# Wider loads for batch 1, later expert weights and additive masks in a fused attention and maxout kernel

## The chip, the cores and the metric

The kernel runs on one core of one Trainium2 chip. The metric is the device time of one execution in microseconds (us), and a version counts as faster or slower when it differs by more than 2%. Two runs of the kernel before took 212.20 and 213.75 us, median 212.97. A profile of one execution comes with each version; its span is 1.7 to 2.1 us shorter than the time of the same execution. The mean TensorE clock that was granted over the span is given as a share of full speed; its record begins only with the first change that it notes, at about 18 us in the changed kernel, and the stretch before counts as full.

Names used throughout: PE is the matmul engine (TensorE), PEld its weight loads, DVE is VectorE, ACT is ScalarE, POOL is GpSimd, SP is SyncE, which in this kernel issues every DMA. In the dense layer xs is the attention's result by tokens and xt its transpose; qb and qk are q and k of a pair before and after their transpose.

## The reference

Attention over 4 batches of 8 heads, 768 tokens, head dimension 64. Three heads are full causal ones, five keep only 4 sink tokens and a window of 64. The result, put together to 3072 rows of 512, goes through a dense layer with two experts, whose elementwise maximum is projected back.

```python
scores = scale * np.matmul(q, k.transpose(0, 1, 3, 2))        # q, k, v: (4, 8, 768, 64) float32
stream_keep = causal & (is_sink | in_win)                     # 4 sinks, window 64
mask = np.where(retr[0, :, 0, 0, None, None], full_mask, stream_mask)
scores = np.where(mask[None, :, :, :], scores, -1000000000.0)
scores = scores - np.max(scores, axis=-1, keepdims=True)
a = np.exp(scores)
a = a / (np.sum(a, axis=-1, keepdims=True) + 1e-09)
attn_out = np.matmul(a, v)
x = attn_out.transpose(0, 2, 1, 3).reshape(B * S, H * D)      # (3072, 512)
h1 = x @ w1                                                   # w1, w2: (512, 1024)
h2 = x @ w2
g = np.maximum(h1, h2)
out = g @ w_out                                               # w_out: (1024, 512)
```

The inputs q and k are drawn with a standard deviation of 0.1; this matters once below.

## The kernel before

The kernel works on pairs of heads: four pairs for each batch, sixteen in all, and after each batch's four pairs the dense layer of that batch ("dense(b)"). The dense layer uses max(h1, h2) = h2 + relu(x(w1 - w2)), so it needs `wd` = w1 - w2 and a product `wm` = w2 w_out that is computed once.

The kernel carries a scheduler of its own, `Plan`. Each operation is declared with a cost for each engine that may run it, its dependencies, its buffers, and a priority. `Plan.schedule` plays these costs through once while the program is built, and the order it finds is the fixed order in which each engine then runs its instructions. Engines run in order: if the next instruction is not ready, those behind it wait too (PE's wait of 3.58 us below is a case).

The buffers that matter here:

```python
    ld_t = tl("ld", [128, 2, NB, D], F32, 9)      # landing buffers of q, k, v
    qb_t = tl("qb", [128, 2, NB, 2, D], BF16, 3)  # q, k cast to bf16
    qk_t = tl("qk", [128, 2, S], BF16, 3)         # q, k transposed
    ...
    gt_t = [old(2, 1, FC, GT), old(0, 0, FC, GT), old(0, 1, FC, GT)]
    ot_t = tl("ot", [128, d_model], F32, 3)       # finished output tiles, waiting for their store
    sc_t = psum("sc", 2, 2)
    po_t = psum("po", 2)
    mm_t = psum("mm", 2)                          # PSUM of dense tiles and transposes
```

A pair loads q, k, v, casts q and k, and transposes them. Batch 0 transposes on PE; the others use a DMA transpose. The "(p n)" order gives each partition six tokens in a row (1536 bytes in one piece); "(n p)" gives pieces of one token (256 bytes).

```python
                order, rate = ("(p n)", 0.34) if b == 0 and src is not v else ("(n p)", 0.225)
                ...  # two loads of src, "o {order} d -> p (o n) d"
                cast.append(P.op(f, {"POOL": 0.95, "DVE": 0.62} if r < 1 else {"POOL": 0.95}, loads[i],
                                 [raws[i], qb], prio=r + 0.01 * i))
                if b > 0:
                    continue
                ...  # PE transposes of qb into PSUM, copied to qk by DVE or ACT
            if b > 0:
                tk.append(P.op(lambda e: nc.sync.dma_start_transpose(
                    out=qk.t.rearrange("c i (n p) -> c (i n) p", p=128),
                    in_=qb.t.rearrange("p i n h d -> p (i n h d)")),
                    {"SP": XBAR}, cast, [qb, qk], prio=r - 0.5, size=0.393, rate=0.2))
```

The exponentiated scores are masked by DVE multiplies, in every batch. `wd` is computed by POOL or DVE:

```python
                    if not pointer:
                        def mk(e, a=a, h0=h0, nh=nh, kind=kind, diag=diag):
                            for x, m in mask_pieces(kind, diag, a.t[:, h0:h0 + nh], nh, s0 + h0):
                                V.tensor_mul(out=x, in0=x, in1=m)
            ...
            def f(e, c=c):
                (V if e == "DVE" else nc.gpsimd).tensor_sub(
                    out=wd_bf[:, c, :], in0=w_raw[0][:, c, :], in1=w_raw[1][:, c, :])
            wd_ops.append(P.op(f, {"DVE": 1.3, "POOL": 2.4}, [d_w["w1", c], d_w["w2", c]], prio=48 + c))
```

The dense layer of batches 1 to 3 gets its input by DMA transposes, and each output tile goes from PSUM to an `ot` tile and from there to DRAM, both transposes and stores issued on the same SP queue as the loads:

```python
                    xt_ops[b].append(P.op(lambda e, n0=n0, n1=n1: nc.sync.dma_start_transpose(
                        out=xt[b].t[:, n0:n1].rearrange("c n k p -> c (n k) p"),
                        in_=xs[b].t[:, n0:n1].rearrange("p n d -> p (n d)")),
                        {"SP": XBAR}, norms[b], [xs[b], xt[b]], prio=-5, size=0.393, rate=0.2))
    ...
                    bk, ot = Buf(mm_p), Buf(ot_p)
                    ...  # twelve matmuls into bk
                    o = P.op(lambda e, bk=bk, ot=ot: copy(e, ot.t, bk.t[:, 0]), {"ACT": 0.53, "DVE": 0.69}, [o],
                             [bk, ot], prio=16 + b)
                    P.op(lambda e, ot=ot, r0=r0: nc.sync.dma_start(out=out[r0:r0 + 128, :], in_=ot.t),
                         {"SP": 0.45}, [o], [ot], prio=-10, size=0.262, rate=0.3)
```

## Time and profile before

| | before |
|---|---|
| time, two runs | 212.20 and 213.75 us |
| profiled span, mean granted clock | 211.9 us, 0.932 |
| PE busy | 176.6 us (83%) |
| first PE matmul / first matmul of dense(0) | 13.46 / 56.6 us |
| batch 1's two xt transposes issued | 105.28 and 107.76 us |
| first matmul of dense(1) | 111.2 us |
| last PE matmul ends | 204.8 us |

First the page of the kernel before, in part: busy time of the engines, then the span in 40 equal slices of 5.3 us, each digit the busy share in tenths; PEclk is the granted clock in tenths.

```profile
PE 176.6 (83%) x1460; PEld 94.4 (45%) x1460; DVE 80.1 (38%) x202; ACT 115.9 (55%) x196; POOL 68.2 (32%) x161
...
PE   0038864689799999997879999999999999999960
...
PEclk9999996599999999999556999999999999999995
DMA  5999999999999999999999999951183202112030
...
DMA packets 99118, 38.91 MB, mean 184 GB/s; under 512 B 91920, under 2 KB 93968, under 8 KB 99088
```

Two things can be read off. The DMA row stands at 9 from 5 us until about 138 us: the input stream is saturated for two thirds of the span. And PE is full only where its row shows 9 at full clock; counting slices from 0, there are two holes after PE's start, slices 5 to 10 (27 to 58 us) and 18 to 20 (95 to 111 us), and in or just after both the clock falls to half as well.

The windows view of PE says how much work is missing there. Its columns are the stretch, its length, PE busy time (instructions), granted clock, DMA share and GB/s.

```profile
10.00:20.00 10.00, 5.11 (x39) 1.00 1.14 320
...
30.00:40.00 10.00, 3.69 (x39) 0.65 1.11 261
...
100.00:110.00 10.00, 7.46 (x73) 0.56 1.28 230
110.00:120.00 10.00, 9.70 (x57) 0.75 1.14 230
```

The first hole is made on other engines. The timeline around 29 us (start, duration, engine, line, operation, in brackets the idle time before and what ended it):

```profile
28.82 0.22 DVE L505 TENSOR_TENSOR at<-at,tri 128x128 bf16<-128x128 bf16 x1
...
29.26 6.96 POOL L386 TENSOR_TENSOR wd_bf<-raw 128x1024 bf16<-128x1024 f32 x3
...
29.65 4.33 DVE L505 TENSOR_TENSOR at<-at,tri 128x128 bf16<-128x128 bf16 x2
...
34.04 0.23 PE L514 MATMUL po<-vb,at 128*128 128x65 bf16 x1 [1.78 <-DVE at L505]
```

While POOL subtracts weights, two mask multiplies of a form that took 0.22 us just before take 4.33 us together, and PE waits for them. The second hole belongs to the queue. The timeline of SP, which issues all DMAs in order:

```profile
105.28 1.80 SPq L628 DMA_TRANSPOSE xt<-xs  x1
107.18 0.53 SPq L686 DMA_DIRECT2D out_dram<-ot  x1
107.76 1.47 SPq L628 DMA_TRANSPOSE xt<-xs  x1
```

Dense(1) cannot start before these two transposes have landed, and until it starts PE has only short attention work. From 111.2 us PE is full to its end at 204.8.

### The profile page before, as it was taken

To read this page: it belongs to the slowest core of one execution; us is meant where nothing else is said; L and a number is where in the kernel's file an instruction comes from. 1 tells how busy PE (TensorE), PEld (TensorE's weight loads), DVE (VectorE), ACT (ScalarE), POOL (GpSimd) and SP (SyncE) were. 2 spreads that over 40 slices of the span, in tenths; PEclk is the share of its full clock that TensorE was granted. 3 is DMA by queue.
4 is the path that set the end of the run, shared out by engine and by line. 5 is a ranking of instruction groups with operands and counts; after the bars stand their busy time and mean duration, and the time that the engine had idled before them with its cause. 6 is when DMAs were issued, how large, how long until landed. Compare 5 with 4: busy or idle time off the path is not lost.

```text
span 211.9 us, 4178 instructions
## 1 busy us (share of the span) xinstructions
PE 176.6 (83%) x1460; PEld 94.4 (45%) x1460; DVE 80.1 (38%) x202; ACT 115.9 (55%) x196; POOL 68.2 (32%) x161
## 2 busy tenths in 40 slices
PE   0038864689799999997879999999999999999960
PEld 0024641545445446545455454545554554545420
DVE  6523799935524563515662035364700000000000
ACT  2088894137385875649553476878472442725320
POOL 6007769929801476243282406120000000000000
PEclk9999996599999999999556999999999999999995
DMA  5999999999999999999999999951183202112030
GB/s 167 404 321 314 357 391 246 221 200 227 209 180 209 236 178 247 242 203 225 192 260 235 232 180 218 212 120 54 49 152 101 99 0 99 53 49 99 14 114 34
DMA packets 99118, 38.91 MB, mean 184 GB/s; under 512 B 91920, under 2 KB 93968, under 8 KB 99088
## 3 DMA queue, kind: packets, MB, share of 16 engines
q1 hardware_dynamic: 99088, 38.55, 82.2%
q8 instruction: 13, 0.21, 0.4%
q14 instruction: 17, 0.14, 0.2%
HBM read 25.17 MB, written 6.29 MB: 148 GB/s over the span
## 4 chain that ended last, share of the span: by engine, by line
PE 69%; DVE 8%; ACT 4%; issue 4%; DVEq 0%; ACTq 0%
PE mm L655 15%; PE mm L673 12%; PE po L514 6%; PE sc L479 6%; PE mm L679 6%; PE po L673 5%; PE sc L655 3%; PE mm L406 3%; DVE at L505 3%; PE po L655 2%; PE po L679 2%; PE sc L673 2%; DVE as_all L505 2%; ACT at L497 2%; ACT as_all L497 2%
## 5 line engine op out<-in xcount | busy, mean ns | idle before, releaser
L497 ACT ACTIVATE at<-sc 128x1024 bf16<-128x1024 f32 (+3 forms) x48 | 33.7, 743 | 7.1 <-PE sc L479 6.5
L655 PE MATMUL mm<-xt,wd_bf 128*128 128x384 bf16 x180 | 35.1, 338 | 0.1
L273 POOL CAST qb<-ld 128x384 bf16<-128x384 f32 x60 | 32.1, 573 | 3.8 <-DMA ld<-in_q_dram 2.0
L655 PEld LDWEIGHTS <-wd_bf 128*128 128x128 bf16 x256 | 24.8, 100 | 18.9 <-issue 4.3
L497 ACT ACTIVATE as_all<-sc 128x896 bf16<-128x896 f32 (+5 forms) x36 | 24.5, 711 | 8.9 <-PE sc L479 8.7
L673 PE MATMUL mm<-wo_bf,raw 128*128 128x512 bf16 x120 | 29.4, 379 | 0.0
L273 POOL CAST vb<-ld 128x384 bf16<-128x384 f32 x32 | 16.2, 533 | 38.6 <-PE po L514 17.1
L505 DVE TENSOR_TENSOR as_all<-as_all,smk 128x384 bf16<-128x384 bf16 (+4 forms) x44 | 20.8, 498 | 20.6 <-ACT as_all L497 20.1
L479 PE MATMUL sc<-qk 64*128 64x192 bf16 (+4 forms) x216 | 25.0, 295 | 2.9 <-ACT as_all L497 1.2
L673 PEld LDWEIGHTS <-raw 128*128 128x128 bf16 x192 | 17.7, 98 | 19.6 <-issue 0.7
L662 ACT ACTIVATE raw<-mm 128x384 bf16<-128x384 f32 x37 | 18.2, 493 | 12.5 <-PE mm L655 11.5
L505 DVE TENSOR_TENSOR at<-at,tri 128x256 bf16<-128x256 bf16 (+1 forms) x48 | 17.1, 364 | 17.4 <-ACT at L497 17.3
L514 PE MATMUL po<-vb,at 128*128 128x65 bf16 x252 | 15.8, 204 | 4.3 <-DVE at L505 4.3
L271 ACT COPY ot<-mm 128x512 f32<-128x512 f32 x14 | 8.2, 587 | 19.8 <-PE mm L679 17.4
L538 DVE TENSOR_TENSOR xs<-po,rz 128x384 f32 x32 | 17.8, 557 | 1.5 <-DVE rz L537 0.4
L582 PE MATMUL mm<-ident,qb 128*128 128x128 bf16 x48 | 5.4, 268 | 14.2 <-DVE qb L273 13.8
L479 PEld LDWEIGHTS <-qk 64*128 64x128 bf16 x216 | 9.3, 97 | 16.7 <-issue 12.8
L514 PEld LDWEIGHTS <-at 128*128 128x128 bf16 x252 | 11.5, 104 | 11.5 <-DVE at L505 7.0
L514 PE MATMUL po<-vb,as_all 128*128 128x65 bf16 x220 | 13.3, 206 | 3.4 <-DVE as_all L505 3.3
L679 PE MATMUL mm<-wm_bf,xt 128*128 128x512 bf16 x60 | 15.4, 380 | 0.0
L514 PEld LDWEIGHTS <-as_all 128*128 128x128 bf16 x220 | 10.5, 105 | 8.9 <-DVE as_all L505 4.8
L679 PEld LDWEIGHTS <-xt 128*128 128x128 bf16 x96 | 8.7, 98 | 9.9 <-issue 0.4
(75 smaller groups left out, 169.4 us busy)
## 6 DMA issues: line engine op xcount, KB each, us to landing
ld<-in_q_dram SPq DMA_DIRECT2D x32, 192.0 KB, 4.3
ld<-in_k_dram SPq DMA_DIRECT2D x32, 192.0 KB, 4.3
ld<-in_v_dram SPq DMA_DIRECT2D x32, 192.0 KB, 4.2
out_dram<-ot SPq DMA_DIRECT2D x24, 256.0 KB, 2.0
raw<-in_moe_w_dram SPq DMA_DIRECT2D x8, 512.0 KB, 7.8
raw<-in_moe_w_out_dram SPq DMA_DIRECT2D x4, 512.0 KB, 5.4
qk<-qb SPq DMA_TRANSPOSE x12, 4.9
xt<-xs SPq DMA_TRANSPOSE x6, 3.8
```

The costliest lines, as they stand in the source:

```text
L271: nc.scalar.copy(out=o, in_=i)
L273: (V if e == "DVE" else nc.gpsimd).tensor_copy(out=o, in_=i)
L406: nc.tensor.matmul(bk.t[:, 0], lhsT=w2t[:, f, c * 128:(c + 1) * 128], rhs=wo_bf[:, f, :], start=(f == 0), stop=(f == FC - 1))
L479: nc.tensor.matmul(sc.t[:, h, off:off + w], lhsT=qk.t[64 * h:64 * h + 64, 1, j * 128:(j + 1) * 128], rhs=qk.t[64 * h:64 * h + 64, 0, q0:q0 ...
L497: nc.scalar.activation(out=view(a.t[:, h:h + m]), in_=view(sc.t[:, h:h + m]), func=ACT.Exp, scale=scale, bias=0.0 if bias is None else bia ...
L505: V.tensor_mul(out=x, in0=x, in1=m)
L514: nc.tensor.matmul(po[h].t[:, 0, i * (D + 1):(i + 1) * (D + 1)], lhsT=a.t[:, h, off + t * 128:off + (t + 1) * 128], rhs=vb.t[:, h, j, :], ...
L538: V.tensor_tensor(out=xs[b].t[:, :, bass.ds(col(s0 + h), D)], in0=p3[:, :, 0:D], in1=rz.t.unsqueeze(2).to_broadcast([128, NB, D]), op=ALU. ...
L655: nc.tensor.matmul(bk.t[:, 0, 0:GT], lhsT=wd_bf[:, c, f * 128:(f + 1) * 128], rhs=xt[b].t[:, g * NB // NG:(g + 1) * NB // NG, c, :], start ...
L662: nc.scalar.activation(out=gt.t[:, f, :], in_=bk.t[:, 0, 0:GT], func=ACT.Relu)
L673: nc.tensor.matmul(bk.t[:, 0], lhsT=gt.t[:, f, t * 128:(t + 1) * 128], rhs=wo_bf[:, f, :], start=(f == 0), stop=False)
L679: nc.tensor.matmul(bk.t[:, 0], lhsT=xt[b].t[:, c0 // 128, c, :], rhs=wm_bf[:, c, :], start=False, stop=(c == KC - 1))
```

## The change

The intent is to take work off the saturated DMA queue and off the engines that starve PE early on:

- Batch 1's q and k load in 1536-byte rows as batch 0's do, and are transposed on PE; four of the twelve DMA transposes of q and k disappear.
- w2 leaves the front of the queue. w1 and w2 load in column halves, w1 behind pair 3, and dense(0)'s first half needs only the first half of `wd`.
- Batch 0's masks are added in PSUM: after the score matmuls, a matmul of the identity with a tile of large negative numbers adds to the scores what the exponential turns to zero. Batch 0 then needs no mask multiplies on DVE.
- Smaller: batch 0's casts may run on DVE, one of the three `gt` buffers gets memory of its own, and some costs and priorities that the planner uses are new.

The core of the diff (cuts marked with three dots):

```diff
+WIDE, NARROW = 0.33, 0.215
+WIDE_TO, MASK_TO, X_BAR = 2, 1, 1
...
-    gt_t = [old(2, 1, FC, GT), old(0, 0, FC, GT), old(0, 1, FC, GT)]
+    gt_t = [tl("gt", [128, FC, GT]), old(2, 1, FC, GT), old(0, 0, FC, GT)]
...
+    def quarter(c):
+        return (slice(c % 2 * KC // 2, (c % 2 + 1) * KC // 2), slice(c // 2 * d_ff // 2, (c // 2 + 1) * d_ff // 2))
+
-    EARLY = (("wo", 0), ("wo", 1), ("wo", 2), ("wo", 3), ("w2", 0), ("w2", 1))
+    EARLY = (("wo", 0), ("wo", 1), ("wo", 2), ("wo", 3))
+    LATER = {("w2", 0): 1.5, ("w2", 1): 1.51, ("w2", 2): 1.52, ("w2", 3): 1.53,
+             ("w1", 0): 3.5, ("w1", 1): 3.51, ("w1", 2): 3.52, ("w1", 3): 3.53}
...
+                by_pe = exact and b < MASK_TO
...
-                                                 start=True, stop=True, skip_group_check=True)
+                                                 start=i == 0, stop=not by_pe, skip_group_check=True)
...
+                def drop(e, hs=hs, steps=steps, sc=sc, score=score):
+                    score(e)
+                    for h in hs:
+                        kind, _, n, diag = steps[h]
+                        for o, m in negatives(kind, diag):
+                            nc.tensor.matmul(sc.t[:, h, o:o + m.shape[-1]], lhsT=ident, rhs=m,
+                                             start=False, stop=True, skip_group_check=True)
...
-                    if not pointer:
+                    if not pointer and not by_pe:
                         def mk(e, a=a, h0=h0, nh=nh, kind=kind, diag=diag):
...
-                order, rate = ("(p n)", 0.34) if b == 0 and src is not v else ("(n p)", 0.225)
+                order, rate = ("(p n)", WIDE) if b < WIDE_TO and src is not v else ("(n p)", NARROW)
...
-                if b > 0:
+                if b >= WIDE_TO:
                     continue
...
-            if b > 0:
+            if b >= WIDE_TO:
                 tk.append(P.op(lambda e: nc.sync.dma_start_transpose(
```

`WIDE_TO` and `MASK_TO` are the number of batches with wide loads and with masks in PSUM.

More of the change, by code (lines that the diff above doesn't have):

```diff
@@ L19 @@
     __slots__ = ("emit", "cost", "deps", "bufs", "prio", "size", "rate", "left", "users",
-                 "ready", "engine", "start", "end", "done", "rows", "then")
+                 "ready", "engine", "start", "end", "done", "rows", "rows_after", "then")
     def __init__(self, emit, cost, deps, bufs, prio, size, rate):
@@ L28, in __init__ @@
         self.engine = self.start = self.end = self.done = None
-        self.rows, self.then = 128, None
+        self.rows, self.rows_after, self.then = 128, None, None
 class Buf:
@@ L70, in schedule @@
         clock = dict.fromkeys(ready, 0.0)
-        dma = 0.0
+        dma = DMA_START
         rows = 128
@@ L123, in schedule @@
                 o.end += SWITCH if o.rows != rows else 0.0
-                rows = o.rows
+                rows = o.rows_after or o.rows
             clock[e] = o.end
@@ L154, in u_engine_differs @@
     return o.size or list(u.cost) != [e]
-W_PRIO = 2.5
-XBAR = 2.6
+XBAR = 2.4
+DMA_START = 0.0
+WIDE, NARROW = 0.33, 0.215
+WIDE_TO, MASK_TO, X_BAR = 2, 1, 1
 @with_exitstack
@@ L231 @@
     bias_0 = tl("bias_0", [128, H], F32)
-    warm = tl("warm", [128, 1], F32)
     tri = tl("tri", [128, 128])
     smk = tl("smk", [128, 448 + 320])
+    ntri = rel[:, 0:64].bitcast(BF16)
+    nsmk = tl("nsmk", [128, 448 + 320])
     w2_bf = tl("w2_bf", [128, KC, d_ff])
@@ L275, in load_weight @@
     def load_weight(name, c):
-        dst, arr, n = {"w1": (w_raw[0], moe_w1, KC // 4), "w2": (w_raw[1], moe_w2, KC // 4),
-                       "wo": (w_raw[2], moe_w_out, FC // 4)}[name]
-        nc.sync.dma_start(out=dst[:, c * n:(c + 1) * n, :],
-                          in_=arr[c * 128 * n:(c + 1) * 128 * n, :].rearrange("(c p) f -> p c f", p=128))
-    EARLY = (("wo", 0), ("wo", 1), ("wo", 2), ("wo", 3), ("w2", 0), ("w2", 1))
+        dst, arr = {"w1": (w_raw[0], moe_w1), "w2": (w_raw[1], moe_w2), "wo": (w_raw[2], moe_w_out)}[name]
+        if name == "wo":
+            rows, cols = slice(c * FC // 4, (c + 1) * FC // 4), slice(0, d_model)
+        else:
+            rows, cols = quarter(c)
+        nc.sync.dma_start(out=dst[:, rows, cols],
+                          in_=arr[rows.start * 128:rows.stop * 128, cols].rearrange("(c p) f -> p c f", p=128))
+    def quarter(c):
[3 more added lines that the diff above has]
+             ("w1", 0): 3.5, ("w1", 1): 3.51, ("w1", 2): 3.52, ("w1", 3): 3.53}
     with tc.manual_schedule():
@@ L291 @@
         V.memset(one, 1.0)
-        nc.scalar.activation(out=warm, in_=one[:, 0:1], func=ACT.Exp, scale=1.0, bias=0.0)
+        nc.scalar.activation(out=nsf[:, 0:1], in_=one[:, 0:1], func=ACT.Exp, scale=1.0, bias=0.0)
         V.tensor_scalar(out=ident, in0=rel[:, 0:128], scalar1=0.0, scalar2=None, op0=ALU.is_equal)
@@ L357, in f @@
                 V.tensor_copy(out=smk[:, 576:768], in_=smk[:, 256:448])
-            c_m = P.op(f, {"DVE": 1.0}, prio=-20)
+                for m, o in ((tri, ntri), (smk, nsmk)):
+                    V.tensor_scalar(out=o, in0=m, scalar1=1.0, scalar2=-NEG, op0=ALU.subtract, op1=ALU.mult)
+            c_m = P.op(f, {"DVE": 1.8}, prio=-20)
         else:
@@ L371, in run @@
         d_w = {}
-        for i, name in enumerate(("w2", "w1")):
+        for name in ("w2", "w1"):
             for c in range(4):
@@ L375, in run @@
                     lambda e, name=name, c=c: load_weight(name, c), {"SP": 0.5},
-                    prio=W_PRIO + 0.1 * i + 0.01 * c, size=0.524, rate=0.36)
+                    prio=LATER[name, c], size=0.524, rate=0.35)
         wd_ops, w2_ops, wo_ops, wm_ops, w2t_ops = [], [], [], [], []
         for c in range(4):
-            w2_ops.append(P.op(lambda e, c=c: copy(e, w2_bf[:, c, :], w_raw[1][:, c, :]),
+            w2_ops.append(P.op(lambda e, c=c: copy(e, w2_bf[(slice(None),) + quarter(c)], w_raw[1][(slice(None),) + quarter(c)]),
                                {"DVE": 0.62, "ACT": 0.95}, [d_w["w2", c]], prio=40 + c))
@@ L385, in f @@
             def f(e, c=c):
-                (V if e == "DVE" else nc.gpsimd).tensor_sub(
-                    out=wd_bf[:, c, :], in0=w_raw[0][:, c, :], in1=w_raw[1][:, c, :])
-            wd_ops.append(P.op(f, {"DVE": 1.3, "POOL": 2.4}, [d_w["w1", c], d_w["w2", c]], prio=48 + c))
+                at = (slice(None),) + quarter(c)
+                (V if e == "DVE" else nc.gpsimd).tensor_sub(out=wd_bf[at], in0=w_raw[0][at], in1=w_raw[1][at])
+            wd_ops.append(P.op(f, {"DVE": 1.3, "POOL": 2.4}, [d_w["w1", c], d_w["w2", c]], prio=30 + c))
         for fch in range(FC):
@@ L396, in tr @@
                                         w2_bf[:, c, fch * 128:(fch + 1) * 128], ident)
-            o = P.op(tr, {"PE": 0.23}, w2_ops, [bk], prio=300 + fch)
+            o = P.op(tr, {"PE": 0.23}, w2_ops[2 * (fch // 4):2 * (fch // 4) + 2], [bk], prio=300 + fch)
             w2t_ops.append(P.op(lambda e, fch=fch, bk=bk: copy(e, w2t[:, fch, :], bk.t[:, 0].bitcast(BF16)[:, 0:d_model]),
@@ L449, in mask_pieces, with negatives @@
             return []
+        def negatives(kind, diag):
+            if kind == "tri":
+                return [(o, ntri) for o in diag]
+            if kind == "band1":
+                return [(256 * m, nsmk[:, 256:448]) for m in range(2)]
+            return [(0, nsmk[:, 0:448] if kind == "band0" else nsmk[:, 448:768])]
         def attend(b, p, qk, vb, tk, ov, sink, r):
@@ L481, in score @@
                                                  rhs=qk.t[64 * h:64 * h + 64, 0, q0:q0 + w],
-                                                 start=True, stop=True, skip_group_check=True)
+                                                 start=i == 0, stop=not by_pe, skip_group_check=True)
                 cols = max(sum(g[2] for g in steps[h][1]) for h in hs)
-                so = score_op(score, cols / 2400 + 0.01, tk, [qk, sc], pr)
-                so.rows = 64
+                def drop(e, hs=hs, steps=steps, sc=sc, score=score):
[5 more added lines that the diff above has]
+                                             start=False, stop=True, skip_group_check=True)
+                extra = sum(m.shape[-1] for h in hs for o, m in negatives(steps[h][0], steps[h][3])) if by_pe else 0
+                so = score_op(drop if by_pe else score, cols / 2400 + 0.01 + (extra / 2400 + SWITCH if by_pe else 0),
+                              tk + ([c_m] if by_pe else []), [qk, sc], pr)
+                so.rows, so.rows_after = 64, 128 if by_pe else 64
                 ready = {}
@@ L544, in tok @@
             return t.rearrange("c (p n) -> c p n", n=NB)
-        def blk(t):
-            return t.rearrange("c (n p) -> c p n", p=128)
         def pair(b, p):
@@ L572, in f @@
                         copy(e, qb.t[:, i, :, h, :], raws[i].t[:, h])
-                cast.append(P.op(f, {"POOL": 0.95, "DVE": 0.62} if r < 1 else {"POOL": 0.95}, loads[i],
+                cast.append(P.op(f, {"POOL": 0.95, "DVE": 0.62} if b == 0 else {"POOL": 0.95}, loads[i],
                                  [raws[i], qb], prio=r + 0.01 * i))
-                if b > 0:
+                if b >= WIDE_TO:
                     continue
@@ L584, in pair @@
                 o = P.op(tr, {"PE": 0.34}, [cast[i]], [qb, bk, qk], prio=90 + 2 * r)
-                tk.append(P.op(lambda e, bk=bk, i=i: copy(e, tok(qk.t[:, i]), blk(bk.t[:, 0].bitcast(BF16)[:, 0:S])),
+                tk.append(P.op(lambda e, bk=bk, i=i: copy(
+                    e, tok(qk.t[:, i]), bk.t[:, 0].bitcast(BF16)[:, 0:S].rearrange("c (n p) -> c p n", p=128)),
                                {"DVE": 0.95, "ACT": 0.8}, [o], [bk, qk], prio=r))
-            if b > 0:
+            if b >= WIDE_TO:
                 tk.append(P.op(lambda e: nc.sync.dma_start_transpose(
@@ L594, in fv @@
                     copy(e, vb.t[:, h, :, 0:D], raws[2].t[:, h])
-            ov = P.op(fv, {"POOL": 0.95}, loads[2],
+            ov = P.op(fv, {"POOL": 0.95, "DVE": 0.7} if b == 0 else {"POOL": 0.95}, loads[2],
                       [raws[2], vb], prio=r + 0.05)
@@ L624, in x_turn @@
         def x_turn(b):
-            if b > 0:
+            if b >= X_BAR:
                 for g in range(NG):
@@ L657, in up @@
                                              start=(c == 0), stop=(c == KC - 1))
-                    o = P.op(up, {"PE": 0.65}, (xt_ops[b][g:g + 1] if b > 0 else xt_ops[b]) + wd_ops + wo_ops, [bk, gt, xt[b]], prio=1000 + 100 * b + 10 * g)
+                    o = P.op(up, {"PE": 0.65}, (xt_ops[b][g:g + 1] if b >= X_BAR else xt_ops[b]) +
+                             (wd_ops[2 * (f // 4):2 * (f // 4) + 2] + wo_ops if b == 0 else wd_ops + wo_ops + w2t_ops), [bk, gt, xt[b]], prio=1000 + 100 * b + 10 * g)
                     def relu(e, f=f, bk=bk, gt=gt):
```

## The prediction

> **What bounds the kernel now.** Three stages, by the windows view and the timeline.
>
> 1. To 56.6 us: batch 0's attention and the weights. PE starts at 13.5 us (first wait: the qb cast of pair 0, behind 3.1 MB of weights); the first dense matmul runs at 56.6. PE idles in between: POOL is busy from 29.3 to 36.2 us with three wd subtractions, while two DVE mask multiplies of 128x128 last 4.3 us together (0.22 each just before), and pair 3's casts queue behind them. The Trainium skill, "GPSIMD Engine Reference" (Specifications), says the SBUF interface is shared with VectorE instructions with two SBUF inputs; the trace agrees.
> 2. 56.6 to 93.4: PE is full (dense(0) plus batch 1's attention). 93.4 to 111.4: PE stutters, at half clock from about 101 to 115. Dense(1) waits for two DMA transposes xt, issued at 105.3 and 107.8 on an SP queue saturated with loads since 5 us (DMA line at 9 until 138 us).
> 3. 111.4 to 204.8: PE full (93 us), then a 7 us tail.
>
> So the chain is: DMA stream to 108 us, then PE to the end.
>
> **What the change moves.**
> - Batch 1's q, k load as 1536-byte rows. The trace's DMA records give about 0.36 MB/us for such packets (batch 0) and 0.21 for 256-byte ones; "DMA: Bandwidth & Descriptors" (Specifications) asks for at least 512 B for line rate, and the trace agrees. 3.15 MB: 15 us become 8.8, minus 6.
> - Four qk DMA transposes vanish: about 2.3 to 2.8 us of queue each (timeline of SP), minus 9 to 10. PE does 48 transposes instead (8 x 0.35 us = 2.8 us), ACT and DVE eight copies of 0.8 to 0.95 us.
> - w2 leaves the front (1 MB, 2.6 us: PE starts near 10.5), w1 moves behind pair 3; wd then follows pair 3's casts on POOL.
> - Batch 0 loses its DVE masks (about 10 us busy, more under contention) and gains about 38 identity matmuls of 8064 columns: 3.4 us at full clock, 4 to 5 with switches. PE is not full there, so little of it shows.
>
> **The sum.** The queue reaches the xt transposes about 16 us earlier (near 90 us, not 106). On PE I estimate batch 0 normalised near 39, dense(0) from about 53 with pairs 0 and 1 of batch 1 done. Dense(0) (26 us), four interleaved pairs (11 us) and about 5 us of waits for batch 2's qk transposes put dense(1) at about 95 instead of 111.4. From there the work left is that of before (93 us) plus one pair (2 us), minus 2 us of half clock: PE ends near 188, tail 7, span about 195. Times run 1 us over the span.
>
> Predicted: **196 us**, 8 in 10 within **189 to 204**; faster by over 2%: 0.93, within 2%: 0.05, slower: 0.02.
>
> **What would show each step right.** Twelve qk transposes become 8; batch 1's xt is issued at 86 to 90. First PE matmul near 10.5. Dense(0)'s first matmul near 53, after pairs 0 and 1 of batch 1. DVE busy falls by 8 to 12 us. PE busy rises by 4 to 6 us at equal clock. From dense(1) on PE is full.
>
> **What would make it wrong.** POOL takes about 4.1 us per pair (six 0.51 us casts, small copies), no less than a wide pair's 4.1 us on DMA: if DVE traffic stretches it, it holds load buffers and delays everything (200 or more). If PE's in-order queue meets batch 1's transposes before POOL's casts, dense(0) starts late. If the waits for batch 2's qk vanish, 190. If PE drops to half clock before dense(0), add 2 to 4 us.

## The result, and the profile after

The changed kernel took 203.13 and 203.71 us, median 203.42. The ratio of the times is 0.9546, with a 95% interval of 0.9476 to 0.9617: faster by 4.5%. Ratios here and below are the mean time of one kernel's runs over that of the other's of the same rounds, so they are not quite the ratio of the medians quoted. Executions over 1.5% slower than the fastest of the same kernel are left out of the means.

| | before | after | predicted |
|---|---|---|---|
| time, median | 212.97 | 203.42 us | 196 (189 to 204) |
| span, mean clock | 211.9, 0.932 | 201.2, 0.978 | about 195 |
| first PE matmul | 13.46 | 10.89 us | near 10.5 |
| first matmul of dense(0) | 56.6 | 57.3 us | near 53 |
| xt of batch 1 issued | 105.28, 107.76 | 84.79, 87.89 us | 86 to 90 |
| first matmul of dense(1) | 111.2 | 95.0 us | about 95 |
| PE ends | 204.8 | 195.9 us | near 188 |
| from dense(1) to PE's end | 93.5 | 100.9 us | 93 |
| DVE busy | 80.1 | 80.6 us | 68 to 72 |
| PE busy | 176.6 | 175.3 us | plus 4 to 6 at equal clock |

The page after, the same lines; a slice is 5.0 us now.

```profile
PE 175.3 (87%) x1546; PEld 95.2 (47%) x1546; DVE 80.6 (40%) x204; ACT 113.6 (56%) x192; POOL 62.5 (31%) x150
...
PE   0049889989999999999999289999999999999990
...
PEclk9999999999999999999999859999999999999997
DMA  4999999999999999999999999901931202112021
...
DMA packets 83630, 37.34 MB, mean 186 GB/s; under 512 B 73360, under 2 KB 77456, under 8 KB 83600
```

Both old holes have nearly closed, and 18,560 packets under 512 bytes are gone (91,920 less 73,360). But a new hole stands at slices 22 and 23 (111 to 121 us), with the clock at half behind it. The windows view:

```profile
10.00:20.00 10.00, 7.09 (x71) 1.00 1.09 305
...
30.00:40.00 10.00, 9.72 (x125) 1.00 1.04 323
...
100.00:110.00 10.00, 9.71 (x108) 1.00 1.22 219
110.00:120.00 10.00, 5.72 (x37) 0.69 1.12 226
```

The timeline of PE in the new hole:

```profile
94.13 1.03 PE L710 MATMUL mm<-wm_bf,xt 128*128 128x512 bf16 x4
95.00 2.30 PE L685 MATMUL mm<-xt,wd_bf 128*128 128x384 bf16 x12
...
109.92 1.03 PE L710 MATMUL mm<-wm_bf,xt 128*128 128x512 bf16 x4
114.53 1.03 PE L502 MATMUL sc<-qk 64*128 64x512 bf16 x6 [3.58 <-DMA qk<-qb]
116.26 0.61 PE L502 MATMUL sc<-qk 64*128 64x512 bf16 x2 [0.69 <-ACT at L529]
116.80 1.89 PE L704 MATMUL mm<-wo_bf,raw 128*128 128x512 bf16 x4
```

PE stands still for 3.58 us, waiting for the DMA transpose of batch 3's first pair, and works at half speed after that: four matmuls of the dense layer take 1.89 us at 116.8, where four took 1.03 just before. The clock record of the trace shows half clock for 6.83 us. The Trainium skill, "TensorE: Matmul & The Clock Gate" (Part 1: The HAM clock gate), says that the gate halves the clock after at least one idle window of about 3.4 us and restores it after a busy one; the wait of 3.58 us and the 6.83 us, two such windows, agree. The kernel before does not: its record falls to half at 33.0 us, after 3.4 us in which PE was busy for 34% of the time, and at 101.3 us, after 3.4 us in which it was busy for 66% and since 93 us no single wait had lasted more than 0.5 us. So in these traces a PE that only stutters loses the clock too.

What SP did meanwhile:

```profile
84.79 2.42 SPq L658 DMA_TRANSPOSE xt<-xs  x1
...
107.79 1.65 SPq L590 DMA_DIRECT2D ld<-in_k_dram  x2
109.54 2.98 SPq L618 DMA_TRANSPOSE qk<-qb  x1
112.64 0.52 SPq L717 DMA_DIRECT2D out_dram<-ot  x1
...
114.58 0.96 SPq L717 DMA_DIRECT2D out_dram<-ot  x2
```

The transpose that PE waits for was issued at 109.54 behind the loads of k, which SP issues as fast as the saturated queue takes them. The stores of three output tiles come at 112.64 and 114.58, although the last of the copies into these tiles had started at 95.2. So all three `ot` tiles are still full when the next dense tile is done, as the timeline of DVE shows:

```profile
115.19 0.69 DVE L276 COPY ot<-mm 128x512 f32<-128x512 f32 x1 [4.58 <-DMA out_dram<-ot]
```

That copy frees a PSUM bank. Until then both `mm` banks hold finished tiles (PE ended them at about 107.2 and 110.9 us, and they are copied at 115.19 and 118.17), so PE has no bank for more dense work. Two readings are possible, and the experiments separate them. In theory A the tiles themselves hold PE up at run time: stores come late, banks stay full. In theory B the damage is done in the plan: the scheduler knew that there are only three `ot` tiles, so it ordered the next attention scores ahead of the next dense tile on PE, and these scores need a transpose that the saturated queue delivers late. The queue is a partner in both.

### The profile page after: what moved, and what is told of

The parts are those of the page before. It is cut to its first block, busy times and chain, and to the rows that moved or that the text cites. A ratio compares the mean times of both kernels' runs of the same rounds, so it can differ in the third digit from the quotient of the medians.

```text
span 201.2 us, 4321 instructions
## 1 busy us (share of the span) xinstructions
PE 175.3 (87%) x1546; PEld 95.2 (47%) x1546; DVE 80.6 (40%) x204; ACT 113.6 (56%) x192; POOL 62.5 (31%) x150
## 2 busy tenths in 40 slices
DMA packets 83630, 37.34 MB, mean 186 GB/s; under 512 B 73360, under 2 KB 77456, under 8 KB 83600
## 4 chain that ended last, share of the span: by engine, by line
PE 70%; DMA 13%; ACT 4%; issue 4%; DVE 3%; POOL 1%; SPq 1%; DVEq 0%; POOLq 0%; ACTq 0%
PE mm L704 10%; PE mm L685 10%; PE sc L502 9%; PE po L546 7%; DMA qk<-qb 6%; PE po L704 4%; PE mm L710 4%; PE sc L685 4%; DMA ld<-in_k_dram 4%; PE mm L420 4%; PE sc L704 3%; PE mm L611 3%; PE po L685 3%; PE sc L512 2%; PE po L710 2%
## 5 line engine op out<-in xcount | busy, mean ns | idle before, releaser
L685 PE MATMUL mm<-xt,wd_bf 128*128 128x384 bf16 x172 | 33.9, 326 | 0.0
L276 POOL CAST qb<-ld 128x384 bf16<-128x384 f32 x54 | 28.9, 557 | 15.8 <-DMA qk<-qb 6.3
L685 PEld LDWEIGHTS <-wd_bf 128*128 128x128 bf16 x256 | 23.5, 98 | 16.3 <-issue 1.3
L276 POOL CAST vb<-ld 128x384 bf16<-128x384 f32 x28 | 14.4, 535 | 23.9 <-DMA ld<-in_v_dram 15.3
L611 PE MATMUL mm<-ident,qb 128*128 128x128 bf16 x96 | 9.0, 237 | 12.7 <-DVE qb L276 12.0
L704 PE MATMUL mm<-wo_bf,raw 128*128 128x512 bf16 x72 | 18.4, 393 | 0.0
L704 PEld LDWEIGHTS <-raw 128*128 128x128 bf16 x120 | 11.2, 99 | 13.6 <-issue 1.8
L537 DVE TENSOR_TENSOR as_all<-as_all,smk 128x384 bf16<-128x384 bf16 (+4 forms) x33 | 15.8, 509 | 2.9 <-ACT as_all L529 2.7
L710 PEld LDWEIGHTS <-xt 128*128 128x128 bf16 x96 | 9.0, 98 | 10.3
L611 PEld LDWEIGHTS <-qb 128*128 128x128 bf16 x96 | 6.7, 107 | 14.3 <-DVE qb L276 12.3
L537 DVE TENSOR_TENSOR at<-at,tri 128x256 bf16<-128x256 bf16 (+1 forms) x36 | 10.3, 296 | 7.6 <-ACT at L529 7.6
```

What stands on the lines that cost most here:

```text
L276: (V if e == "DVE" else nc.gpsimd).tensor_copy(out=o, in_=i)
L611: nc.tensor.transpose(psb[:, n * 128:(n + 1) * 128], qb.t[:, i, n].rearrange("p h d -> p (h d)"), ident)
L685: nc.tensor.matmul(bk.t[:, 0, 0:GT], lhsT=wd_bf[:, c, f * 128:(f + 1) * 128], rhs=xt[b].t[:, g * NB // NG:(g + 1) * NB // NG, c, :], start ...
L704: nc.tensor.matmul(bk.t[:, 0], lhsT=gt.t[:, f, t * 128:(t + 1) * 128], rhs=wo_bf[:, f, :], start=(f == 0), stop=False)
L710: nc.tensor.matmul(bk.t[:, 0], lhsT=xt[b].t[:, c0 // 128, c, :], rhs=wm_bf[:, c, :], start=False, stop=(c == KC - 1))
```

## The experiments

Each kernel ran four times, beside the kernel before on the same chip. All gave the reference's result except two that are wrong. Medians in us.

| run | what | median | ratio to before, 95% | correct |
|---|---|---|---|---|
| (after) | the change | 203.42 | 0.9546 (0.9476 to 0.9617) | yes |
| ot8 | after + 8 output tiles | 196.32 | 0.9229 (0.9175 to 0.9283) | yes |
| late_wide_addr | after, batches 2, 3 in wide rows | 197.38 | 0.9257 (0.9221 to 0.9293) | no |
| u_masks | after, old masks | 203.14 | 0.9502 (0.9445 to 0.9560) | yes |
| u_narrow1 | after, batch 1 as before | 213.50 | 0.9970 (0.9896 to 1.0045) | yes |
| ot8_same_order | after's order, 8 tiles at run time | 202.68 | 0.9478 (0.9425 to 0.9532) | yes |
| b_ot8 | before + 8 output tiles | 213.34 | 1.0001 (0.9969 to 1.0034) | yes |
| ot8_masks | ot8, old masks | 200.42 | 0.9437 (0.9372 to 0.9503) | yes |
| u_weights | after, weights about as before | 206.95 | 0.9711 (0.9688 to 0.9734) | yes |
| b1_narrow_addr | after, batch 1 in narrow rows | 208.70 | 0.9792 (0.9735 to 0.9848) | yes |
| ot8_no_ident | ot8 without the mask matmuls | 196.12 | 0.9211 (0.9174 to 0.9247) | no |
| w3_ot8 | ot8, batch 2 wide too | 202.40 | 0.9501 (0.9470 to 0.9533) | yes |
| b_wide | before + wide batch 1 | 204.90 | 0.9610 (0.9584 to 0.9637) | yes |

### ot8: more output tiles

The fp32 copy of w2 is dead once `wd` exists, so five more tiles cost no memory.

```diff
     ot_t = tl("ot", [128, d_model], F32, 3)
+    ot_t += [raw[:, 1, 512 * i:512 * (i + 1)] for i in range(5)]
```

> The changed kernel with 8 instead of 3 output tiles (five more lie in the dead w2 area); the planner orders anew. It tests why PE stands still from 110.9 to 114.5 us of the changed kernel, in front of the scores of batch 3's pair 0. Theory A (the load queue alone): the qk transpose lands late and nothing else matters; output tiles change nothing, 203.4 us within 1. Theory B (output ring): dense tiles could have filled the gap, but their PSUM banks are held because copies into the 3 output tiles wait for stores that sit in the queue behind prefetched loads; with 8 tiles PE fills the gap, its wait for DMA falls from 3.6 us to under 1, no half clock after 100 us, about 196 to 199 us.

Measured: 196.32 us, and the mean clock rises to 0.994. The timeline of PE:

```profile
109.78 1.03 PE L711 MATMUL mm<-wm_bf,xt 128*128 128x512 bf16 x4
110.64 1.89 PE L705 MATMUL mm<-wo_bf,raw 128*128 128x512 bf16 x8
112.37 1.03 PE L711 MATMUL mm<-wm_bf,xt 128*128 128x512 bf16 x4
113.23 2.30 PE L686 MATMUL mm<-xt,wd_bf 128*128 128x384 bf16 x12
115.77 0.61 PE L503 MATMUL sc<-qk 64*128 64x512 bf16 x6 [0.23 <-DMA qk<-qb]
```

The scores come no earlier than in the changed kernel (115.77 us against 114.53); what differs is that a dense tile and twelve more dense matmuls now stand before them in PE's order and fill the gap. The late wait and the half clock behind it are worth 7.1 us by the medians, nearly all of the distance between the prediction and the result. By the ratios it is 6.8 us. This does not yet tell theory A from B, since the number of tiles changed both the plan and the run.

### ot8_same_order: the tiles without the new order

Here the scheduler still plans with three tiles, so all orders are those of the changed kernel, but the copies and stores use eight tiles in turn.

```diff
+    ot_x = ot_t + [raw[:, 1, 512 * i:512 * (i + 1)] for i in range(5)]
...
+                    ox = ot_x[(b * S + c0) // 128 % 8]
-                    o = P.op(lambda e, bk=bk, ot=ot: copy(e, ot.t, bk.t[:, 0]), ...
+                    o = P.op(lambda e, bk=bk, ox=ox: copy(e, ox, bk.t[:, 0]), ...
-                    P.op(lambda e, ot=ot, r0=r0: nc.sync.dma_start(out=out[r0:r0 + 128, :], in_=ot.t),
+                    P.op(lambda e, ox=ox, r0=r0: nc.sync.dma_start(out=out[r0:r0 + 128, :], in_=ox),
```

> The changed kernel's own planned order on every engine (planned with 3 output tiles), but the copies and stores go round 8 tiles. ot8 gained 7 us; this tells whether by the tiles at run time or by the order that the planner makes with them. Theory (order): PE's queue still has the scores of batch 3's pair 0 next at 110.9 us, and PE takes its instructions in turn, so it still waits about 3.6 us for the qk transpose: 203.4 within 1.5 us; the DVE wait of 4.6 us for a store vanishes all the same. Rival (run-time ring): 196 to 198 us.

Measured: 202.68 us, less than the changed kernel by 0.7 us by the medians and 1.4 by the ratios, whose intervals overlap. DVE's wait for a store is gone, and PE's wait is not:

```profile
110.78 1.03 PE L712 MATMUL mm<-wm_bf,xt 128*128 128x512 bf16 x4
114.88 0.61 PE L503 MATMUL sc<-qk 64*128 64x512 bf16 x6 [3.08 <-DMA qk<-qb]
116.39 0.39 PE L503 MATMUL sc<-qk 64*128 64x512 bf16 x2 [0.90 <-ACT at L530]
116.71 1.89 PE L706 MATMUL mm<-wo_bf,raw 128*128 128x512 bf16 x4
```

One of the four runs took 200.70 us at a full clock. So theory A falls and theory B stands: free tiles at run time gain little, the order that the scheduler makes when it knows of them gains 5 to 6 us (5.3 by the ratios 0.9478 and 0.9229 to the kernel before, 6.4 by the medians). Whether that order would gain as much with three tiles at run time was not run.

### late_wide_addr: the same order on a queue with room

The order of every engine and the number of bytes stay; batches 2 and 3 fetch q, k and v in wide rows. The result is wrong (tokens land in the wrong places).

```diff
+                    at_ = order if b < 2 else "(p n)"
-                    two.append(P.op(lambda e, t=t, src=src, h=h, order=order: nc.sync.dma_start(
+                    two.append(P.op(lambda e, t=t, src=src, h=h, order=at_: nc.sync.dma_start(
```

> Wrong result on purpose, same planned order on every engine: q, k, v of batches 2 and 3 are read with 1536-byte rows instead of 256-byte rows (same bytes, same issues). It tests whether the saturated queue causes the wait at 110.9 us at all. Theories A and B: 9.4 MB at about 0.36 instead of 0.21 MB/us, the queue runs 15 us or more ahead by batch 3, the 3.6 us wait and the half clock after it vanish: minus 7 us, about 196 us. Rival C (PE's in-order queue, ACT and DVE latencies decide the rest): within 2 us of 203.4.

Measured: 197.38 us; PE waits for no transpose around 110 us (its scores start at 111.34 straight after the dense tile), and the clock is 0.998:

```profile
110.38 1.03 PE L711 MATMUL mm<-wm_bf,xt 128*128 128x512 bf16 x4
111.34 0.61 PE L502 MATMUL sc<-qk 64*128 64x512 bf16 x6
```

The saturated queue is thus the other half of the cause: with three tiles and the same order, a queue that keeps up removes the wait too.

### b_ot8: the same tiles in the kernel before

```diff
     ot_t = tl("ot", [128, d_model], F32, 3)      # in the kernel before
+    ot_t += [raw[:, 1, 512 * i:512 * (i + 1)] for i in range(5)]
```

> The kernel before with 8 output tiles, planned anew. Theory: before, dense(1) itself waited for the xt transposes until 111.4 us and dense(0) was finished by 94, so no dense work was there to fill with: within 2 us of 213. Rival: the output ring was as dear before, and 8 tiles give 5 us or more there too: 208 or less.

Measured: 213.34 us, a ratio of 1.0001. Three tiles cost nothing in the kernel before. They became a limit only in the changed kernel's plan, where dense(1) starts 16 us sooner. The move alone is not enough: `b_wide` and `u_weights` below also have three tiles and start dense(1) at 98.97 and 97.43 us, and from there to the end their PE stands idle for 0.00 and 0.85 us, against 4.57 in the changed kernel. So the late wait belongs to the order that the scheduler found here. More tiles remove it, but so do other changes that make it plan anew; why three tiles lead to this order in one plan and not in another was not looked into.

### u_narrow1: batch 1 as before

```diff
-WIDE_TO, MASK_TO, X_BAR = 2, 1, 1
+WIDE_TO, MASK_TO, X_BAR = 1, 1, 1
```

> The changed kernel with batch 1 back on 256-byte rows and DMA transposes; weights and masks stay changed, the planner orders anew. Theory: the gain is the queue time saved (about 11 us in the records: inputs end at 130 instead of 140 us), so nearly all of it goes: 211 to 215 us, 12 qk transposes, inputs end near 140 us. Rival: the weight order and the masks carry the gain: 204 to 207 us.

Measured: 213.50 us over its fast and slow runs, a ratio of 0.997 over the fast ones (one of four, 215.36 us, was slow). Without the wide loads the rest of the change gains nothing. Batch 0 gets through sooner, dense(0) starts at 47.7 us instead of 57.3, but then PE has to wait for the queue: xt of batch 1 is issued at 105.7, as in the kernel before, and there are waits of 2.16 and 2.30 us for qk transposes at 91.7 and 107.3, with half clock from 87.2 to 97.5 and from 100.9 to 114.5. An engine that comes sooner to a queue that does not only waits longer.

### b_wide: the wide loads alone, in the kernel before

```diff
-                order, rate = ("(p n)", 0.34) if b == 0 and src is not v else ("(n p)", 0.225)
+                order, rate = ("(p n)", 0.34) if b < 2 and src is not v else ("(n p)", 0.225)
-                if b > 0:
+                if b > 1:
                     continue
...
-            if b > 0:
+            if b > 1:
                 tk.append(P.op(lambda e: nc.sync.dma_start_transpose(
```

> The kernel before with batch 1's q, k wide and transposed on PE, nothing else of the change. Undone one at a time, the wide loads were worth 10 us, the weight order 3.5, the masks nothing. Theory: the parts lean on one another (without the weight order PE starts at 13.5 us and the wd work still blocks POOL near 30 us), so alone the wide loads give 4 to 8 us: 205 to 209. Rival: additive, 203 within 1.

Measured: 204.90 us. The wide loads alone bring 8 of the change's 9.5 us, at the upper edge of what I thought or just beyond it. The remaining 1.5 us is not clear of noise: the intervals 0.9584 to 0.9637 and 0.9476 to 0.9617 overlap. The last load of v is issued at 109.5 us here, against 125.1 before: 15.6 us less queue. In the changed kernel it is issued at 114.0, a gain of 11.1; the other parts of the change give 4.5 us of it back. Part of that lies in the rows of the weights: halved columns leave 2048 bytes where w1 and w2 had 4096, and the packets of those two sizes occupy the sixteen engines for 36.3 us against 33.7 before (sum of packet times over 16). The rest was not looked into.

### b1_narrow_addr: rows or transposes

The wide loads of batch 1 do two things: longer rows, and four fewer DMA transposes. Here the rows are narrow again and the PE transposes stay.

```diff
+                    at_ = "(n p)" if b == 1 else order
-                    two.append(P.op(lambda e, t=t, src=src, h=h, order=order: nc.sync.dma_start(
+                    two.append(P.op(lambda e, t=t, src=src, h=h, order=at_: nc.sync.dma_start(
```

> Wrong result on purpose, the changed kernel's order on every engine: batch 1's q, k are read in 256-byte rows again, while the transposes stay on PE. It parts the wider rows from the dropped DMA transposes (together worth 10 us, by u_narrow1). Theory: both are queue time, and the rows are about 6 us of it (3.15 MB at 0.36 or 0.21 MB/us), which lengthens the late wait one for one: 208 to 211 us. Rival: the rows lie in slack, the four dropped transposes carry the gain: 205 or less.

Measured: 208.70 us. The page counts 85,648 packets under 512 bytes, 12,288 more than in the changed kernel, which is 3.15 MB in pieces of 256 bytes, so the edit did what it should. The result was meant to be wrong, since tokens of batch 1 come in a permuted order, but passed; I think that is because q and k are so small that the softmax is nearly even, which I did not test. The time stands halfway: 203.42, 208.70, 213.50 for wide rows, narrow rows, and narrow rows with DMA transposes, and the last load of v is issued at 114.0, 119.3 and 125.9 us. Longer rows are worth about 5.3 us and the dropped transposes 4 to 5 (4.8 by the medians, 3.8 by the ratios). The second figure also holds what `u_narrow1` loses or gains by being planned anew; `b1_narrow_addr` keeps the changed kernel's order.

### u_masks and ot8_masks: the masks back on DVE

```diff
-WIDE_TO, MASK_TO, X_BAR = 2, 1, 1
+WIDE_TO, MASK_TO, X_BAR = 2, 0, 1
```

> The changed kernel with batch 0's masks back on DVE (no identity matmuls); the planner orders anew. Theory: batch 0's masks are nearly off the chain, because dense(0) waits for the loads of batch 1 and for wd on POOL: within 1.5 us of 203.4. Rival: DVE masks with two SBUF inputs collide with POOL's casts and wd as before, batch 0 ends 3 us or more later and holds up loads: 206 or more. DVE busy rises by about 10 us, PE busy falls by about 4.

Measured: 203.14 us. In the changed kernel the masks in PSUM gain nothing. DVE busy goes up by 5.2 us (to 85.8), and batch 0 does run later: dense(0) starts at 64.6 us instead of 57.3. But by 120 us that is made up: this run has no wait for the late transpose, only 0.96 us for ACT at 119. So the same edit was made where the late wait is gone:

> ot8 with batch 0's masks back on DVE. With the late wait, the masks were worth nothing (203.1 against 203.4), perhaps because that wait swallowed whatever the first 60 us gained. Theory 1: with the wait gone the earlier dense(0) counts, ot8 without identity matmuls is slower: 198 to 202. Theory 2: the PE then bounds, and the identity matmuls' 3.4 us is about what they save: within 1.5 us of 196.3.

Measured: 200.42 us against 196.32. Here the masks in PSUM are worth 4 us. PE waits 2.67 us for a POOL copy at 38.3 us and has two spells of half clock, 3.4 us each, from 24.5 and 38.1 us. In `u_masks` the same loss at the front had been offset: its new order was spared the late wait that the changed kernel has. So a part of the change that is worth something seemed worthless.

### ot8_no_ident: what the mask matmuls cost PE

The other side of the same trade: ot8's order with the identity matmuls left out.

```diff
+    ot_t += [raw[:, 1, 512 * i:512 * (i + 1)] for i in range(5)]
...
                     score(e)
+                    return
...
-                                                 start=i == 0, stop=not by_pe, skip_group_check=True)
+                                                 start=i == 0, stop=True, skip_group_check=True)
```

> Wrong result on purpose: ot8's order, but batch 0's 38 identity matmuls are not emitted and nothing masks there. It prices the identity matmuls where the late wait no longer hides them. Theory: ot8 is bound by PE from 15 us on, so their PE time shows, 3 to 4.5 us: 192 to 193.5 us. Rival: they fill gaps in the first 40 us and cost nothing: 196.3 within 1 us.

Measured: 196.12 us, within 0.2 us of ot8. My theory that PE is the bound everywhere in ot8, so that its matmuls must cost time, falls. PE busy between 30 and 40 us drops from 9.65 to 7.86 us, and nothing ends sooner: the identity matmuls fill time in which PE would wait for something else. The trace without them even has a spell of half clock (0.85 in that window) that ot8 has not.

### u_weights: the weights about as before

```diff
-    EARLY = (("wo", 0), ("wo", 1), ("wo", 2), ("wo", 3))
-    LATER = {("w2", 0): 1.5, ("w2", 1): 1.51, ("w2", 2): 1.52, ("w2", 3): 1.53,
-             ("w1", 0): 3.5, ("w1", 1): 3.51, ("w1", 2): 3.52, ("w1", 3): 3.53}
+    EARLY = (("wo", 0), ("wo", 1), ("wo", 2), ("wo", 3), ("w2", 0), ("w2", 1))
+    LATER = {("w2", 2): 2.52, ("w2", 3): 2.53,
+             ("w1", 0): 2.6, ("w1", 1): 2.61, ("w1", 2): 2.62, ("w1", 3): 2.63}
```

> The changed kernel with half of w2 back in front and the rest of w2 and w1 behind pair 2 (three output tiles). PE then starts near 13.5 us instead of 10.9. Theory: all before the queue-bound part of batches 2 and 3 is slack, since the loads in total are the same bytes: the late wait remains and the time stays within 2 us of 203.4. Rival: the weight order carries 3 us or more: 206 or more.

Measured: 206.95 us, 3.5 us slower than the changed kernel; I had taken the start of the span for slack, and that was wrong. The first scores run at 19.60 us instead of 14.55, PE is busy for 4.05 us between 10 and 20 us instead of 7.09, and dense(0) starts at 70.0 us. The late wait is not there in this run, so the loss at the front is larger than the 3.5 us that the time shows.

### w3_ot8: one batch more

```diff
-WIDE_TO, MASK_TO, X_BAR = 2, 1, 1
+WIDE_TO, MASK_TO, X_BAR = 3, 1, 1
...
+    ot_t += [raw[:, 1, 512 * i:512 * (i + 1)] for i in range(5)]
```

> ot8 with batch 2 on wide rows and PE transposes too (a correct kernel). Theory: ot8 is bound by PE and not by the queue any more; another 48 transposes and their waits cost more than the queue time saved buys: 197.5 to 201 us. Rival: the queue still holds PE back somewhere: 193 to 195 us.

Measured: 202.40 us, 6 us slower than ot8, more than expected. The loads end far sooner (the last v load is issued at 99.9 us instead of 114.4), but the queue no longer matters: in ot8 PE is already full from 50 us on. The groups view shows what was added, the transposes of q and k on PE, first in ot8 and then in w3_ot8 (count, busy us, mean ns):

```profile
L612 PE MATMUL mm<-ident,qb 128*128 128x128 bf16 x96 | 9.2, 240 | 12.4 <-DVE qb L277 11.7 <-ACT wm_bf L275 0.3 <-ACT qk L275 0.2
```

```profile
L612 PE MATMUL mm<-ident,qb 128*128 128x128 bf16 x144 | 13.3, 234 | 12.9 <-DVE qb L277 11.8 <-DVE qk L277 0.5 <-ACT wm_bf L275 0.3
```

Forty-eight more transposes cost 4.1 us of PE, where I had counted 2.8. With PE's 1.3 us of new idle time between 60 and 80 us (18.65 us busy there against 19.95), that is 5.4 of the 6 us.

## Why the prediction was right, and where it was not

**Right in direction, by luck in the number: the chain up to dense(1).** The prediction said that the queue would reach the xt transposes near 90 us, and that dense(1) would start at about 95 us instead of 111.4. They were issued at 84.79 and 87.89, and dense(1) started at 95.00. `u_narrow1` shows that this is where the gain comes from: with narrow loads xt goes out at 105.7 us and the whole gain is gone. But the queue no longer sets that start. The second transpose landed at 91.86 us, and PE, idle for only 0.32 us since dense(0) began, went from the last tile of dense(0) straight into dense(1). In the prediction's own sum (53 and 26 and 11 and 5 make 95) dense(0) came 4.3 us later than estimated, and the 5 us of waits for batch 2's qk transposes shrank to those 0.32 us; the work between took 37.4 us, as estimated (37). Two misses cancel, and that the start is 95.0 is luck. The time of 203.42 us lies 0.6 us inside the upper end of the range.

**Wrong: "From dense(1) on PE is full."** This is the step that failed, in the sum as "from there the work left is that of before (93 us)". From dense(1) to the last matmul it took 100.9 us. PE stood still for 3.58 and 0.69 us, and ran at half clock for 6.83 us, of which it was idle for about 1.5, so that about 5.3 us of work at half speed cost some 2.7 more. Together that is 7.0 of the 7.9 us over. `ot8` shows the reason by removing it: with more output tiles in the plan the kernel takes 196.32 us, the number predicted, and 94.3 us from dense(1) at 94.88 to PE's end at 189.18. I had carried the second half of the trace of before over to an earlier time. There the dense layer of batch 1 ran from 111.2 us, with 14 us to go until the last load was issued; moved to 95, it shares the queue with loads for 19 us. Of the output tiles' stores and the next pairs' transposes, nothing was in the sum beyond "about 5 us of waits for batch 2's qk transposes", ahead of dense(1). The prediction gave the risk of half clock only before dense(0).

**Mis-sized: 16 us of queue.** The inputs' last load went out 11.1 us sooner, not 16. The wide loads alone, in `b_wide`, do give 15.6; the rest of the change costs 4.5 of it. The parts were off in both directions: longer rows measured 5.3 us for an estimated 6, and four dropped DMA transposes 4 to 5 in time (6.6 in the issue of the last load) for an estimated 9 to 10. I had costed a transpose by the 2.3 to 2.8 us for which SP issues it. Part of that is waiting for room, but not most: at 154 us of the kernel before, with little else on the queue, SP still takes 1.45 us. The 0.39 MB of a transpose at the 208 GB/s that the windows view shows from 90 to 100 us, among narrow loads, is 1.9 us, an estimate that fits the 6.6 (1.65 each) better.

**Mis-sized: dense(0) near 53.** It started at 57.3, even later than before (56.6). The trace shows PE full from 50 us on with pairs of batch 1 and weight products, so no PE time was lost there: those pairs had to be done anyway.

**Wrong: DVE busy falls by 8 to 12 us.** It went from 80.1 to 80.6. The mask multiplies of batch 0 did leave (in the page's groups, those on full heads fall from 17.1 to 10.3 us and those on windowed heads from 20.8 to 15.8), but DVE took over casts of batch 0 and copies of the new PE transposes, which I had not charged to it. `u_masks`, where they return, has only 5.2 us more of DVE. Nothing hung on it: in this kernel the masks in PSUM are worth nothing, and with the late wait removed 4 us.

**Roughly right: contention of POOL with DVE.** The two multiplies that took 4.33 us beside POOL's subtractions have gone, and PE's busy time between 30 and 40 us rose from 3.69 to 9.72 us. The Trainium skill, "GPSIMD Engine Reference" (1. Specifications), names the shared SBUF interface; the traces agree. In the kernel before the two multiplies take 2.03 and 2.38 us, and each ends 0.08 us after one of POOL's subtractions. DVE's own subtraction of weights, the same in each kernel, took 3.38 us beside a subtraction and a cast on POOL, and 1.21 us in `u_narrow1` at 36.8 us, with POOL all but idle. No run was made to test this alone.

**PE busy.** Predicted to rise at equal clock; it fell by 1.3 us at a mean clock of 0.978 against 0.932. The identity matmuls raise it by about 2 us (175.3 against 173.1 in `u_masks`), and `ot8_no_ident` shows that in ot8's order they cost no time.

Put together, the clock tells the story as well as the busy rows: half clock, as far as it is on record and outside the last microseconds, lasted 23.9 us before, 6.8 after, and 0 in ot8. `ot8` is the best version, 7.7% faster than the kernel before and 3.5% faster than the changed one (196.32 against 203.42).

## What to carry to other kernels

When a change moves a stage forward in time, do not carry its duration over from the old trace: ask what else uses its queue and its buffers at the new time, and above all which instruction stands next in each engine's order if one transfer comes late. A buffer count that is harmless in one schedule can decide the order in the next, and where a planner fixes the order, adding buffers at run time is no remedy; the planner has to know of them. And test a part of a change twice, once as it stands and once with the dominating wait removed, before calling it worthless: the masks here measured 0 us and 4 us.

## What the Trainium skill lacked or had wrong

- "DMA: Bandwidth & Descriptors" (Specifications) asks for at least 512 bytes for line rate, but the page gives no measured rate for loads in shorter rows. Here the saturated queue of the changed kernel moved 215 GB/s in a stretch of 256-byte rows (60 to 80 us) and 322 GB/s where most bytes came in rows of 1536 and 2048 bytes (20 to 40 us); going from one to the other for 3.15 MB saved 5.3 us.
- The same page has a bandwidth for DMA transposes, but not what an SBUF-to-SBUF transpose of 0.39 MB takes from a saturated queue. Four of them fewer moved the last load by 6.6 us, 1.65 each, though `u_narrow1` was also planned anew; that is about what a load in 256-byte rows of the same size costs (0.39 MB at 215 GB/s is 1.8 us, an estimate).
- "Perfetto Trace Analysis" (DMA Optimizations) advises to issue inputs and outputs from separate engines, but no page shows what stores on SP behind prefetched loads can cost: three output tiles, the last copied at 95.2 us, were not stored before 112.6 to 115.2 us.
- "TensorE: Matmul & The Clock Gate" (Part 1) has the clock halved after at least one idle window of about 3.4 us. The changed kernel fits, with 6.83 us of half clock after a wait of 3.58 us; the kernel before does not, where the clock fell at 101.3 us although PE had been busy for 66% of the 3.4 us before.
- The same page, Part 4, gives about 275 ns for one PE transpose in a kernel. Duration is not cost: here one lasts 234 to 240 ns in the profile, but 48 more in a row of pipelined ones added 4.1 us of PE time, 85 ns each.
- No page has the cost of masks added by identity matmuls: 38 of them in batch 0 cost 0.2 us of time (196.32 against 196.12), and spared 4 us of mask multiplies (200.42).
